# Attention and two MoE layers in one kernel: the second MoE with four pairs of chunks by seven products, groups of 4, 4 and 8, integer turns for the cosine, and half the second sums added by DMA

## The chip, the core and the metric

The kernel is written in Bass and Tile for Trainium2 and runs on one core. A core has TensorE (PE, matmuls; PEld is its weight load), VectorE (DVE), ScalarE (ACT), GpSimd (POOL) and SyncE (SP, which here only starts transfers). The metric is the time of one execution on the device, in microseconds; lower is better.

## What is computed

Causal attention with a decay bias over 4 batches, 8 heads and 576 positions gives 2304 tokens of 512 numbers. They go through two layers with a hidden width of 2048. Only the second is changed:

```python
def _moe_ref(x, w_in, w_out):
    h = np.maximum(x @ w_in, 0.0)
    return (h * h @ w_out).astype(np.float32)

def _moe2_ref(x, w_in, w_out):
    h = x @ w_in
    g = h * np.cos(h)
    return (g @ w_out).astype(np.float32)
```

with w_in 512 x 2048 and w_out 2048 x 512.

## The kernel before

The order of all instructions is written out by hand (`manual_schedule`): each engine runs its instructions in the order in which the program emits them.

**The second MoE.** The 2304 tokens are cut into blocks 0 to 4 (`blocks`: four of 512 tokens, the last of 256), the hidden width into 16 chunks f of 128. A value is kept as a high and a low half of 16 bits, so a product of two values is three matmuls (`PASSES`). `m2_g1(j, f)` multiplies block j by the columns of chunk f: 12 matmuls of 512 columns (256 for block 4) into the PSUM tile hp. `m2_cos` and `m2_sin` make cos(h) from it as a sine of whole turns removed, `m2_mul` multiplies by h, `m2_high` and `m2_rest` split the result g into gh and gl. `m2_g2` multiplies g by chunk f of w_out: for each 128 tokens a of the block 3 matmuls of 512 columns into PSUM tile o0 to o3.

**Groups.** Chunks are worked off in three groups (`GROUPS`, here numbered 1 to 3; in the code p = 0, 1, 2). Within a group all blocks are done one after the other. After the last chunk of a group for a block, the four o tiles are evicted, scaled by `osc`: group 1 writes them to the tiles `part` in SBUF, group 2 adds to these (four times on DVE, line 1678), group 3 adds the rest (o0 and o2 on DVE; o1 and o3 by ACT into `os` and POOL's addition, line 1684) and stores the rows. `part[c]` and `half[c]` are the two halves of the tile that holds weight entry c.

**Pairs.** From chunk `PAIR0` on, blocks 0 to 3 take two chunks at once, in `unit`: a scheme of seven products of half-sized blocks instead of eight (`PROD`), each 6 matmuls of 256 columns into a PSUM bank. `snap` copies a bank to SBUF on ACT, `join` adds a bank to it on DVE. Product 6 adds to the bank that was snapped after product 1, product 5 to that, product 3 to that; so each waits for the snap before. Block 4 takes all its chunks singly. The combined columns of the weights are made by `pair_high` (additions on DVE into the tile `sums`, conversions on ACT) and `w_lo`; the combined rows of the tokens by `t_make`, a few instructions at each `t_tick`.

**The loop** goes over `items`, one chunk (or pair) of one block each. An item emits `m2_g1` of its chunk, the cosine, the high half of the item before, weight conversion, the sine, the low half (gl) of the item before, then `m2_g2` of the chunk two items back (`fifo`, `G2LAG`), then more weight conversion and the multiplication. A unit has two places for output products: `first` and `second` are the oldest chunks in the fifo, each cut into `out_part(x, 0)` (its first half of the o tiles) and `out_part(x, 1)`.

**Weights.** The queue `wq` lists 64 entries, 32 of them of the second MoE: (1, f, a), a = 0 for w_in, 1 for w_out. An entry is loaded, clipped on ACT (line 975), shifted and combined on DVE (lines 981 and 985), squared on ACT for its scale, and then converted to a high half on ACT (1008, 1034) and a low half on DVE (1051, 1042). `goal` says how many entries shall have passed line 985 by item i; eight are done when the second MoE begins, and the rate is `P_BITS`, later `LATE_BITS`, per item. In the first MoE's last block the raw entries are loaded as that layer's weights come free, at each of its output chunks f except even ones from `PAIR0` on.

Of the kernel before, what the change touches and what calls it, by code (L numbers as in the profile page):

```python
# [30 lines left out]
GROUPS = ((0, 4), (4, 9), (9, 16))  # L31
PAIR0 = 10
T_FROM = 20
LATE_BITS = 0.62
RAWS = 6
NB2 = 5
LAG = (3, 5)
# [78 lines left out]
P_BITS = 0.75  # L116
QUIET = 3
PAUSE = 14
# [14 lines left out]
def attention_moe_moe_kernel(  # L133
# [64 lines left out]
    wq += [(1, f + m, a) for f in range(PAIR0, NF, 2) for a in range(2) for m in range(2)]  # L198
# [811 lines left out]
    def pair_high(j, m):  # L1010
# [5 lines left out]
        if m == 0:  # L1016
            q = p2q[0].tile([128, KD, BT], F32, tag="yr", bufs=2, name="sums")
# [493 lines left out]
    for k in range(NB1):  # L1511
# [41 lines left out]
        if k == NB1 - 2:  # L1553
# [6 lines left out]
            for name, shape, t in (  # L1560
                ("onesb", [128, 128], BF16),
                ("wss", [128, 2 * NF], F32),
# [17 lines left out]
            nc.vector.memset(sm["onesb"], 1.0)  # L1580
            nc.vector.memset(sm["ysm"], 0.0)
# [34 lines left out]
    def m2_cos(j, f, p=2):  # L1616
        n = blocks[j][1]
        hp = hd2[j, f]
        a = p2.tile([128, n], F32, tag="a", bufs=2, name="a")
        kf = p2.tile([128, n], F32, tag="kf", bufs=2, name="kf")  # L1620
        nc.scalar.activation(out=a, in_=hp, func=ACTF.Copy, scale=sm["hsc"][:, j, f:f + 1], bias=0.25)
        if p == 1:
            nc.scalar.activation(out=kf, in_=a, func=ACTF.Copy, bias=MAGIC)
            nc.vector.scalar_tensor_tensor(
                out=kf, in0=kf, scalar=MAGIC, in1=a, op0=ALU.subtract, op1=ALU.subtract
            )
            hd2[j, f] = (hp, a, kf)
            return
        nc.vector.tensor_scalar(out=kf, in0=a, scalar1=MAGIC, scalar2=MAGIC, op0=ALU.add, op1=ALU.subtract)
        nc.vector.tensor_tensor(out=kf, in0=kf, in1=a, op=ALU.subtract)  # L1630
        hd2[j, f] = (hp, a, kf)

    def m2_sin(j, f):
        hp, a, kf = hd2[j, f]
        nc.scalar.activation(out=a, in_=kf, func=ACTF.Sin, scale=-6.2831850)  # L1635
        hd2[j, f] = (hp, a)
# [22 lines left out]
    def m2_g2(p, j, f, pick=None):  # L1659
# [4 lines left out]
        sc = sm["osc"][:, p, j:j + 1]  # L1664
        if first:
            ops.setdefault(j, {})
        for a in range(n // 128) if pick is None else pick:
# [7 lines left out]
            if last:  # L1675
                st = part[4 * j + a]
                if p == 1 or p and (a % 2 == 0 or j == NB2 - 1):
# [3 lines left out]
                elif p:  # L1681
                    os = p2.tile([128, DM], F32, tag="os", bufs=2, name="os")
# [102 lines left out]
    def unit(j, f, prev):  # L1785
# [23 lines left out]
        if old:  # L1809
            m2_high(*old[0])  # L1810
            m2_mul(*old[1])
# [39 lines left out]
    for i, (kind, p, j, f) in enumerate(items):  # L1851
# [33 lines left out]
        if i > G2LAG and prev[0] == "f":  # L1885
            m2_rest(*prev[1:])
# [76 lines left out]
```

## Time and profile before

| | |
|---|---|
| median of 3 runs | 972.91 us (971.38 to 973.18) |
| the profiled execution | 972.91 us, span of its instructions 970.8 us |
| PE busy | 937.3 us, 97% |
| DVE busy | 769.7 us, 79% |
| ACT busy | 709.7 us, 73% |
| POOL busy | 159.9 us, 16% |
| second MoE | first hp matmul at 595.2 us, last o matmul at 965.4 us |

The span runs from the first instruction to the last; the execution takes some 2 us more. Matmuls are pipelined: a matmul's own duration overlaps that of the next, so what the PE needs for one is read from the distance between starts, or from a piece of the chain that counts several.

### The profile page before, as it was taken

To read this page: it belongs to the slowest core of one execution; us is meant where nothing else is said; L and a number is where in the kernel's file an instruction comes from. 1 tells how busy PE (TensorE), PEld (TensorE's weight loads), DVE (VectorE), ACT (ScalarE), POOL (GpSimd) and SP (SyncE) were. 2 spreads that over 40 slices of the span, in tenths; PEclk is the share of its full clock that TensorE was granted. 3 is DMA by queue.
4 is the path that set the end of the run, shared out by engine and by line. 5 is a ranking of instruction groups with operands and counts; after the bars stand their busy time and mean duration, and the time that the engine had idled before them with its cause. 6 is when DMAs were issued, how large, how long until landed. Compare 5 with 4: busy or idle time off the path is not lost.

```text
span 970.8 us, 21039 instructions
## 1 busy us (share of the span) xinstructions
PE 937.3 (97%) x7474; PEld 726.9 (75%) x7474; DVE 769.7 (79%) x1944; ACT 709.7 (73%) x1625; POOL 159.9 (16%) x298
## 2 busy tenths in 40 slices
PE   6999999989999999999999999999999999999997
PEld 5899998988989988999989986445544456666664
DVE  6899986789798866787997375888788788798774
ACT  6799887878898767676776686677777666565553
POOL 2001123222211222222330022430000000001101
PEclk9999999999999999999999999999999999999999
DMA  8984799657998987589999679210000000112001
GB/s 246 312 271 149 168 213 227 168 145 151 200 183 191 204 195 170 134 177 174 211 215 158 217 267 362 66 44 23 1 1 1 22 1 22 49 60 67 23 22 66
DMA packets 158074, 135.38 MB, mean 139 GB/s; under 512 B 109272, under 2 KB 132128, under 8 KB 157968
## 3 DMA queue, kind: packets, MB, share of 16 engines
q1 hardware_dynamic: 147664, 123.78, 50.8%
q0 software_dynamic: 10304, 10.24, 5.2%
q8 instruction: 59, 0.97, 0.4%
q14 instruction: 47, 0.39, 0.1%
HBM read 93.91 MB, written 15.83 MB: 113 GB/s over the span
## 4 chain that ended last, share of the span: by engine, by line
PE 59%; DVE 6%; ACT 3%; issue 2%; DMA 2%; SPq 0%; DVEq 0%; ACTq 0%
PE o L1671 18%; PE hp L1610 12%; PE y L1197 11%; PE hps L1165 9%; PE bank L1762 5%; PE qkp L567 2%; PE pvs L697 2%; DVE k L415 1%; DVE sb L585 1%; DMA raw<-in_qk_dram 1%; DMA rw<-in_w_dram 1%; DMA vb<-v_d 1%; DVE wt L1678 1%; PE xps L752 0%; ACT sb L608 0%
## 5 line engine op out<-in xcount | busy, mean ns | idle before, releaser
L1197 PE MATMUL y<-gh,wt 128*128 128x256 f32 x1152 | 237.7, 289 | 0.0
L1197 PEld LDWEIGHTS y<-gh,wt 128*128 128x128 f32 x1152 | 188.6, 190 | 1.2
L1671 PE MATMUL o<-wt,gh 128*128 128x512 f16 x576 | 171.3, 379 | 1.5 <-ACT gh L1649 1.3
L1197 PE MATMUL y<-gl,wt 128*128 128x256 f32 x576 | 162.9, 283 | 0.5 <-DVE gl L1187 0.5
L1165 PE MATMUL hps<-xh,w 128*128 128x256 f16 x1152 | 142.0, 273 | 2.6 <-ACT g L1177 2.4
L1610 PE MATMUL hp<-yh,wt 128*128 128x512 f16 (+1 forms) x448 | 124.9, 348 | 0.0
L1165 PEld LDWEIGHTS <-w 128*128 128x128 f16 x1152 | 106.1, 98 | 17.8 <-issue 4.2
L1197 PEld LDWEIGHTS y<-gl,wt 128*128 128x128 f32 x576 | 109.9, 191 | 1.4 <-DVE gl L1187 0.9
L1671 PE MATMUL o<-wt,gl 128*128 128x512 f16 x288 | 109.2, 379 | 0.0
L1610 PEld LDWEIGHTS <-wt 128*128 128x128 f16 x672 | 63.9, 98 | 59.1
L1671 PEld LDWEIGHTS <-gh 128*128 128x128 f16 x576 | 56.3, 98 | 56.3 <-ACT gh L1649 1.6
L608 ACT ACTIVATE sb<-sb 128x128 f32<-128x128 f32 (+7 forms) x152 | 87.4, 575 | 4.9 <-DVE sb L585 4.3
L1177 ACT ACTIVATE g<-hps,sc 128x256 f32<-128x256 f32 x96 | 45.1, 470 | 61.3 <-PE hps L1165 59.8
L397 POOL DMA_DIRECT2D k<-ext_d x80 | 41.1, 514 | 260.2 <-PE qkp L567 159.3
L1165 PE MATMUL hps<-xh,wt 128*128 128x256 f32 x384 | 81.4, 294 | 0.3 <-ACT g L1179 0.2
L1187 DVE TENSOR_TENSOR gl<-g,gh 128x256 fp32r<-128x256 f32 x144 | 61.3, 426 | 22.8 <-ACT gh L1181 14.7
L1610 PE MATMUL hp<-yl,wt 128*128 128x512 f16 (+1 forms) x224 | 78.0, 348 | 0.0
L585 DVE CUSTOM_DVE_ANT_0 sb<-qkp,mask 128x128 f32<-128x128 f32 (+7 forms) x152 | 69.3, 456 | 5.3 <-PE qkp L552 4.3
L656 DVE SCALAR_TENSOR_TENSOR p<-sb,p 128x384 f16<-128x384 f32 (+3 forms) x120 | 66.3, 553 | 8.8 <-ACT p L650 5.6
L1635 ACT ACTIVATE a<-kf 128x512 f32<-128x512 f32 (+1 forms) x80 | 46.5, 583 | 31.4 <-DVE kf L1630 30.4
L405 ACT CAST hi<-raw 128x704 fp32r<-128x704 f32 (+2 forms) x80 | 58.8, 735 | 13.6 <-DMA raw<-in_qk_dram 7.2
L1165 PEld LDWEIGHTS hps<-xh,wt 128*128 128x128 f32 x384 | 64.5, 195 | 2.8 <-issue 1.2
(172 smaller groups left out, 2006.8 us busy)
## 6 DMA issues: line engine op xcount, KB each, us to landing
rw<-in_w_dram SPq DMA_DIRECT2D x64, 512.0 KB
raw<-in_qk_dram SPq DMA_DIRECT2D x48, 352.0 KB
yr<-y_d SPq DMA_DIRECT2D x17, 512.0 KB
raw<-in_qk_dram SPq DMA_DIRECT2D x16, 384.0 KB
v_d<-vt SPq DMA_DIRECT2D x16, 320.0 KB
vb<-v_d SPq DMA_DIRECT2D x32, 160.0 KB
vr<-in_v_dram POOLq DMA_DIRECT2D x15, 320.0 KB, 5.4
y_d<-yst SPq DMA_DIRECT2D x18, 256.0 KB
```

What stands on the lines that cost most here:

```text
L405: nc.scalar.copy(hi[:, BT - nq:BT + nk], raw[:, BT - nq:BT + nk])
L585: nc.vector.tensor_tensor_reduce(out=sb[0:r, c0:c0 + cn], in0=p[0:r, 0:cn], in1=mask[0:r, mo:mo + cn], scale=-0.125, scalar=(3.0e38 if k = ...
L608: nc.scalar.activation(out=sb[0:r, 0:w], in_=sb[0:r, 0:w], func=ACTF.Exp, scale=-1.0, bias=j["nb"], accum_out=z[0:r, ti, x:x + 1],)
L656: nc.vector.scalar_tensor_tensor(out=p[0:r, cw:cw + w], in0=sb[0:r, 0:w], scalar=PSC, in1=p[0:r, 0:w], op0=ALU.mult, op1=ALU.subtract,)
L1165: nc.tensor.matmul(hp, w[:, a, c * 128:(c + 1) * 128], (xh, xl)[e][:, c, :], start=(n == 0), stop=(n == 3 * KD - 1),)
L1177: nc.scalar.activation(out=g, in_=hp, func=ACTF.Relu, scale=hs1[:, f // 2:f // 2 + 1])
L1187: nc.vector.tensor_tensor(out=gl, in0=g, in1=gh, op=ALU.subtract)
L1197: nc.tensor.matmul(yps[k][d // 2][:, d % 2, :], w[:, a, d * 128:(d + 1) * 128], (gh, gl)[e], start=(f == 0 and n == 0 and d % 2 == 0), sto ...
L1610: nc.tensor.matmul(hp, chunk_of(w, a, c), (yh, yl)[e][:, c, :], start=(m == 0), stop=(m == 3 * KD - 1),)
L1635: nc.scalar.activation(out=a, in_=kf, func=ACTF.Sin, scale=-6.2831850)
L1671: nc.tensor.matmul(ops[j][a], (gh, gl)[e][:, a * 128:(a + 1) * 128], w[:, x, :], start=(first and m == 0), stop=(last and m == 2),)
L1762: nc.tensor.matmul(bank[b][:, 0:HB], w[:, a, wx, c * 128:(c + 1) * 128], y_side(j, yx, e, c), start=(start and n == 0), stop=(n == 5), ski ...
```

## The change

- `GROUPS` goes from 4, 5, 7 chunks to 4, 4, 8, and `PAIR0` from 10 to 8. So group 3 of blocks 0 to 3 is four pairs, with no single chunk before them.
- The queue of weights takes w_out before w_in for the first pair; `PARTS` names the 18 tiles that hold the partial sums, since chunks 8 and 9 now have such a tile only beside their w_out.
- Weight entries are converted at 1.05 an item in group 1 and 0.68 in group 2, only in blocks 0 to 3, and not in group 3.
- `m2_cos`: ACT writes the number of turns as an integer, one step on DVE subtracts it from the scaled h (two before; in group 2 two ACT steps and one DVE step). The sine takes the quarter turn as a bias tile.
- Evictions are no longer emitted within `m2_g2` but collected in `evq2` and emitted by `m2_evict`, after other work in a unit. In group 2, o1 and o3 of blocks 0 to 3 go by ACT into tile `os` and are added to `part` by an accumulating DMA from POOL's queue; o0 and o2, and block 4, stay on DVE.
- `os` has one buffer in group 3, shared with `sums`; in group 2 it takes the buffers of `yr`.
- In a unit the snap after product 6 comes before the high half of the old chunk, and both ticks of `t_make` after the join of product 5.

```diff
-GROUPS = ((0, 4), (4, 9), (9, 16))
-PAIR0 = 10
+GROUPS = ((0, 4), (4, 8), (8, 16))
+PAIR0 = 8
-LATE_BITS = 0.62
+BITS2 = (1.05, 0.68, 0)
+PARTS = (*range(2 * PAIR0), 2 * PAIR0 + 1, 2 * PAIR0 + 3)
...
-    wq += [(1, f + m, a) for f in range(PAIR0, NF, 2) for a in range(2) for m in range(2)]
+    wq += [(1, f + m, a) for f in range(PAIR0, NF, 2) for a in ((1, 0) if f == PAIR0 else (0, 1)) for m in range(2)]
...
-            q = p2q[0].tile([128, KD, BT], F32, tag="yr", bufs=2, name="sums")
+            q = p2q[1].tile([128, KD, BT], F32, tag="os", bufs=1, name="sums")
...
-    def m2_cos(j, f, p=2):
+    def m2_cos(j, f):
...
+        sc = sm["hsc"][:, j, f:f + 1]
...
-        nc.vector.tensor_scalar(out=kf, in0=a, scalar1=MAGIC, scalar2=MAGIC, op0=ALU.add, op1=ALU.subtract)
-        nc.vector.tensor_tensor(out=kf, in0=kf, in1=a, op=ALU.subtract)
+        kf = p2.tile([128, n], I32, tag="kf", bufs=2, name="kf")
+        nc.scalar.activation(out=kf, in_=hp, func=ACTF.Copy, scale=sc, bias=0.25)
+        nc.vector.scalar_tensor_tensor(out=a, in0=hp, scalar=sc, in1=kf, op0=ALU.mult, op1=ALU.subtract)
...
-        nc.scalar.activation(out=a, in_=kf, func=ACTF.Sin, scale=-6.2831850)
+        nc.scalar.activation(out=a, in_=a, func=ACTF.Sin, scale=6.2831850, bias=sm["hpi"])
...
             if last:
-                st = part[4 * j + a]
-                if p == 1 or p and (a % 2 == 0 or j == NB2 - 1):
+                evq2.append((p, j, f, a))
+    def m2_evict():
+        while evq2:
+            p, j, f, a = evq2.pop(0)
...
+                st = part[PARTS[4 * j + a]]
+                if p and (a % 2 == 0 or j == NB2 - 1):
                     nc.vector.scalar_tensor_tensor(
                         out=st, in0=ops[j][a], scalar=sc, in1=st, op0=ALU.mult, op1=ALU.add
                     )
                 elif p:
...
                     nc.scalar.activation(out=os, in_=ops[j][a], func=ACTF.Copy, scale=sc)
-                    nc.gpsimd.tensor_tensor(out=st, in0=os, in1=st, op=ALU.add)
+                    if p == 1:
+                        nc.gpsimd.dma_start(out=st, in_=os, accum_op=ALU.add)
+                    else:
+                        nc.gpsimd.tensor_tensor(out=st, in0=os, in1=st, op=ALU.add)
...
         join(j, f, 1, 0, 0)
+        m2_evict()
         out_part(first, 0)
...
         prod(j, f, 6, 0, False)
+        snap(j, f, 0, 1, 0)
+        m2_evict()
         if old:
             m2_high(*old[0])
             m2_mul(*old[1])
-        snap(j, f, 0, 1, 0)
         prod(j, f, 7, 2, True)
         out_part(first, 1)
         if old:
             m2_high(*old[1])
             m2_rest(*old[0])
             m2_rest(*old[1])
-            t_tick(j + 1)
         prod(j, f, 5, 0, False)
         snap(j, f, 0, 1, 1)
         join(j, f, 2, 1, 1)
+        m2_evict()
+        if old:
+            t_tick(j + 1)
         out_part(second, 0)
...
-        k = i + 1 - QUIET
-        goal = min(4 * NF, bits0 + int(max(0, min(k, PAUSE)) * P_BITS) + int(max(0, k - PAUSE - 1) * LATE_BITS))
+        if i >= QUIET and j < NB2 - 1:
+            pace[0] += BITS2[p]
+        goal = min(4 * NF, bits0 + int(pace[0]))
```

## Rows read from the trace of the kernel before

**Rows 1.** Busy time by stretch: PE, PEld, DVE, ACT, POOL, clock, DMA share, GB/s

```profile
595.20:683.80 88.60, 88.60 (x442) 42.10 (x441) 72.26 (x129) 61.08 (x118) 21.54 (x17) 1.00 0.24 84
788.00:826.00 38.00, 36.03 (x242) 22.77 (x239) 32.55 (x77) 24.27 (x52) 0.00 (x0) 1.00 0.05 15
826.00:965.80 139.80, 139.57 (x894) 87.16 (x891) 104.88 (x186) 79.79 (x152) 10.11 (x8) 1.00 0.14 46
```

**Rows 2.** Chain of waits: start us, us, what; 512 columns, then 256

```profile
605.75 2.59 PE hp L1610 x12
...
857.99 1.31 PE bank L1762 x12
```

**Rows 3.** Timeline of PE: start us, us, what, idle before

```profile
797.39 0.59 PE L1671 MATMUL o<-wt,gh 128*128 128x512 f16 x2 [0.18 <-DVE wt L1678]
...
799.92 0.27 PE L1610 MATMUL hp<-yh,wt 128*128 128x256 f16 x1
801.52 0.60 PE L1671 MATMUL o<-wt,gh 128*128 128x512 f16 x2 [1.33 <-ACT gh L1649]
...
813.41 0.82 PE L1762 MATMUL bank<-wt,wt 128*128 128x256 f16 x6
814.69 0.27 PE L1762 MATMUL bank<-yh,wt 128*128 128x256 f16 x1 [0.46 <-ACT hs L1772]
...
855.47 0.38 PE L1671 MATMUL o<-wt,gl 128*128 128x512 f16 x1
855.88 0.82 PE L1762 MATMUL bank<-wt,wt 128*128 128x256 f16 x6
```

**Rows 4.** Groups by line and shape in the second MoE: count, busy us, mean ns

```profile
L1656 DVE TENSOR_TENSOR gl<-a,gh 128x512 f16<-128x512 f32 x64 | 44.0, 687 | 3.9 <-ACT gh L1649 2.7
L1630 DVE TENSOR_TENSOR kf<-kf,a 128x512 f32<-128x512 f32 x44 | 36.9, 839 | 1.5
L1641 DVE SCALAR_TENSOR_TENSOR a<-hp,gsc,a 128x512 f32<-128x512 f32 x40 | 29.9, 747 | 8.9 <-ACT a L1635 8.8
L1629 DVE TENSOR_SCALAR kf<-a 128x512 f32<-128x512 f32 x44 | 21.4, 485 | 9.4 <-ACT a L1621 8.3
L1772 ACT COPY hs<-bank 128x256 f32<-128x256 f32 x48 | 17.7, 369 | 27.6 <-PE bank L1762 26.9
L1621 ACT ACTIVATE a<-hs,hsc 128x512 f32<-128x512 f32 x24 | 17.2, 722 | 0.4
L1776 DVE TENSOR_TENSOR hs<-bank,hs 128x256 f32<-128x256 f32 x36 | 15.2, 422 | 20.8 <-ACT hs L1772 10.2 <-PE bank L1762 10.0
L1624 DVE SCALAR_TENSOR_TENSOR kf<-kf,a 128x512 f32<-128x512 f32 x20 | 13.8, 690 | 16.1 <-ACT kf L1623 15.9
L1051 DVE SCALAR_TENSOR_TENSOR wt<-st,wsc,wt 128x512 f16<-128x512 f32 x18 | 12.7, 747 | 0.3 <-ACT wt L1008 0.3
L1623 ACT ACTIVATE kf<-a 128x512 f32<-128x512 f32 x20 | 12.6, 630 | 0.6
L1684 POOL TENSOR_TENSOR wt<-os,wt 128x512 f32<-128x512 f32 x8 | 10.1, 1269 | 287.5 <-ACT os L1683 256.6 <-DVE wt L1708 30.9
```

**Rows 5.** Timeline of DVE: start us, us, the four evictions of block 3, group 2

```profile
796.59 2.72 DVE L1678 SCALAR_TENSOR_TENSOR wt<-o,osc,wt 128x512 f32<-128x512 f32 x4
```

**Rows 6.** Timeline of POOL and of DVE in block 2 of group 1

```profile
643.92 2.65 POOL L1253 TENSOR_TENSOR yl<-yr,yh 128x512 f16<-128x512 f32 x2 [8.29 <-ACT yh L1252]
...
645.49 1.37 DVE L1629 TENSOR_SCALAR kf<-a 128x512 f32<-128x512 f32 x1 [0.38 <-ACT a L1621]
646.89 1.49 DVE L1630 TENSOR_TENSOR kf<-kf,a 128x512 f32<-128x512 f32 x1
```

**Rows 7.** Timeline of ACT and of DVE in group 2: hp taken up, gl made

```profile
722.85 0.69 ACT L1621 ACTIVATE a<-hp,hsc 128x512 f32<-128x512 f32 x1 [2.54 <-PE hp L1610]
...
727.71 0.69 DVE L1656 TENSOR_TENSOR gl<-a,gh 128x512 f16<-128x512 f32 x1
```

**Rows 8.** DMA issues: line, count, KB each, median us to landing

```profile
vr<-in_v_dram POOLq DMA_DIRECT2D x15, 320.0 KB, 5.4
```

More of the change, by code (lines that the diff above doesn't have):

```diff
@@ L1614, in m2_g1 @@
         hd2[j, f] = hp
-    def m2_cos(j, f, p=2):
+    def m2_cos(j, f):
         n = blocks[j][1]
         hp = hd2[j, f]
+        sc = sm["hsc"][:, j, f:f + 1]
         a = p2.tile([128, n], F32, tag="a", bufs=2, name="a")
[L1620 to L1628, printed above, removed]
-        nc.vector.tensor_scalar(out=kf, in0=a, scalar1=MAGIC, scalar2=MAGIC, op0=ALU.add, op1=ALU.subtract)
-        nc.vector.tensor_tensor(out=kf, in0=kf, in1=a, op=ALU.subtract)
-        hd2[j, f] = (hp, a, kf)
+        kf = p2.tile([128, n], I32, tag="kf", bufs=2, name="kf")
+        nc.scalar.activation(out=kf, in_=hp, func=ACTF.Copy, scale=sc, bias=0.25)
+        nc.vector.scalar_tensor_tensor(out=a, in0=hp, scalar=sc, in1=kf, op0=ALU.mult, op1=ALU.subtract)
+        hd2[j, f] = (hp, a)
     def m2_sin(j, f):
-        hp, a, kf = hd2[j, f]
-        nc.scalar.activation(out=a, in_=kf, func=ACTF.Sin, scale=-6.2831850)
-        hd2[j, f] = (hp, a)
+        hp, a = hd2[j, f]
+        nc.scalar.activation(out=a, in_=a, func=ACTF.Sin, scale=6.2831850, bias=sm["hpi"])
     def m2_mul(p, j, f):
@@ L1675, in m2_g2 @@
             if last:
-                st = part[4 * j + a]
-                if p == 1 or p and (a % 2 == 0 or j == NB2 - 1):
+                evq2.append((p, j, f, a))
+    evq2 = []
+    def m2_evict():
+        while evq2:
+            p, j, f, a = evq2.pop(0)
+            t0, n = blocks[j]
+            sc = sm["osc"][:, p, j:j + 1]
+            if True:
+                st = part[PARTS[4 * j + a]]
+                if p and (a % 2 == 0 or j == NB2 - 1):
                     nc.vector.scalar_tensor_tensor(
@@ L1681, in m2_g2 @@
                 elif p:
-                    os = p2.tile([128, DM], F32, tag="os", bufs=2, name="os")
+                    if p == 1:
+                        os = p2q[0].tile([128, KD, BT], F32, tag="yr", bufs=2, name="os")
+                    else:
+                        os = p2.tile([128, KD, BT], F32, tag="os", bufs=1, name="os")
+                    os = os[:, 0:2].rearrange("p a c -> p (a c)")
                     nc.scalar.activation(out=os, in_=ops[j][a], func=ACTF.Copy, scale=sc)
-                    nc.gpsimd.tensor_tensor(out=st, in0=os, in1=st, op=ALU.add)
+                    if p == 1:
+                        nc.gpsimd.dma_start(out=st, in_=os, accum_op=ALU.add)
+                    else:
+                        nc.gpsimd.tensor_tensor(out=st, in0=os, in1=st, op=ALU.add)
                 elif a % 2 == 0:
@@ L1690, in m2_g2 @@
                 for row, x, m in _pieces(t0 + a * 128, 128):
-                    nc.sync.dma_start(out=out[row:row + m, :], in_=part[4 * j + a][x:x + m])
+                    nc.sync.dma_start(out=out[row:row + m, :], in_=part[PARTS[4 * j + a]][x:x + m])
     HB = BT
@@ L1828, in unit @@
         join(j, f, 2, 1, 0)
+        m2_evict()
         for m in range(2):
@@ L1886, in attention_moe_moe_kernel @@
             m2_rest(*prev[1:])
+        m2_evict()
         if len(fifo) >= G2LAG:
             m2_g2(*fifo.pop(0))
+            m2_evict()
         if p == 0 and j + 1 < NB2 and f == 1:
@@ L1913, in attention_moe_moe_kernel @@
         m2_g2(*fifo.pop(0))
+        m2_evict()
 def _lay_out(inputs):
```

9 lines of the change are left out of this document (4 added, 5 removed).

## The prediction

> **What bounds the kernel now.** I read the stretches of the second MoE first, because the change touches nothing else but an order of weight loads. In the first group of chunks the PE is busy in all 88.60 us, from 826 to 965.8 us in 139.57 of 139.80; only between 788 and 826 us does it miss about 2 us (36.03 of 38.00) [rows 1]. The granted clock is 1.00 throughout, the 2.4 GHz level [rows 1], so no time is to be had from the clock. The chain of waits agrees: one piece of PE work follows the other, 2.59 us for twelve matmuls over 512 columns, 1.31 us for twelve over 256 columns [rows 2]. So this stage is worth what its matmuls are worth, plus the places where the PE stands still. DVE (72.26) and ACT (61.08 us of 88.60) matter only where their lateness reaches the PE [rows 1].
>
> I then looked for those places by the spacing of the matmuls' starts. There are three kinds. Around the change from the second to the third group: a 256-column matmul starts at 799.92 and the next only at 801.52, where 0.11 was due, so 1.5 us are lost, and 0.18 before 797.39 [rows 3]; with two slivers beside them some 2.0 us. In the first unit of seven products: at 813.41 six matmuls start (0.66 us of work) and the next starts at 814.69: 0.6 us lost, waiting for ACT's snap [rows 3]. And in one unit of each of three blocks a bank matmul that was due 0.22 after 855.47 starts 0.41 after it: 0.2 us, three times, some 0.6 [rows 3]. Together about 3.2 us, of which the first 2.0 is a jam of DVE: four evictions stand in one row, 2.72 us from 796.59, in items that are only half as long as the others because block 4 has 256 tokens [rows 5].
>
> **The change, part by part.**
>
> *A fourth pair.* For each of blocks 0 to 3, chunks 8 and 9 go from 24 matmuls of 512 columns to 7 x 6 = 42 of 256. At 2.59 and 1.31 per twelve [rows 2] that is 5.18 against 4.585 us: 0.6 us a block, 2.4 us in all, and it lies wholly on the path, since the PE is the path. The output products stay as many. The three pairs of before already run at this spacing, so it is no guess. Each pair adds four snaps (0.369) on ACT and three joins (0.422) on DVE [rows 4], 2.7 us per block, beside 9.8 us of PE in a unit.
>
> *Cosine by integer turns.* In groups 1 and 3 DVE drops a tensor_scalar (0.485) and a tensor_tensor (0.839) for one scalar_tensor_tensor. The trace has none with an int32 operand and a scalar; nearest is the multiplication by the same accumulator, 0.747 [rows 4]; below it the bound is 0.690 (the fused step of group 2), above it 0.839 [rows 4]. I take 0.747: DVE saves 0.58 per chunk of 512. In group 2 ACT drops one pass of 0.630 [rows 4], DVE pays 0.06 more. The sine gets a bias by pointer; the row of a cosine step with a pointer, 0.722 [rows 4], bounds it at 0.1 more than now. None of this is on the path by itself: it shortens the chain from hp to the output product by some 0.5 us a chunk, and the chain has slack already.
>
> The two dropped steps took 1.37 and 1.49 us while POOL worked from 643.92 to 646.57, 0.9 and 0.7 more than their usual time [rows 4, 6]. The Trainium skill's SBUF — State Buffer (Who interferes with whom) says why: a DVE instruction with two SBUF inputs, or in a two-port mode, is shut out for as long as a GpSimd instruction that reads SBUF runs. The trace agrees so far. By that page the new step is free of it in single chunks (hp lies in PSUM) and not in pairs; the sum is the same by either, and what it would do in pairs is rival 2.
>
> *Faster weights.* By item 15 thirteen entries are converted, not nine, and none in group 3. An entry costs DVE three passes, each at most 0.747 (the step of line 1051 [rows 4]), so at most 2.2, and ACT three passes of about 0.72, 2.2 as well. Four more entries are 9 us on each. DVE gets 13 x 0.58 = 7.5 back; ACT gets nothing, and with 61.08 of 88.60 busy it goes to some 80% in blocks 0 to 3. Is that late enough to reach the PE? The item at 722.85 of before measures the slack: its hp was ready then, gl of the chunk before it was made from 727.71 on, and the PE was to use it after two more pieces of 2.59, at about 728.0 [rows 2, 7]. DVE was some 2.2 us behind there, four additions for a pair stood before gl, and no wait of the PE is listed. So an item can bear DVE 3 to 3.6 us behind. The heavy items of group 1 have cosine, multiplication and gl (2.2), two evictions (half of 2.72 [rows 5]), two low halves and two passes for an entry (0.75 each): 6.6 us on DVE against 5.2 of PE; the light ones between them, without evictions and low halves, 3.7. So DVE gets 1.4 behind and takes it back. Tightest are items 17 and 18, half-sized with the first pair's conversion in them: 17 has 1.4 for its own steps, 1.4 of evictions, four additions (0.42) and 1024 columns of low halves (1.5), 6.0 us against 3.9 of PE; 18 has 2.9 against 2.6. That is 2.4 behind, where a half-sized item bears about 2.6. I enter 0.2 us for that place.
>
> *The change from group 2 to group 3.* Entries end before block 4 of group 2, the last pair's conversion lies in items 35 and 36, and of four evictions two go to ACT and a DMA. So the 2.0 us jam goes. Late next is the first unit: it has only one chunk in the fifo to spare, so product 5 is followed at once by product 3, and the same snap as at 814.69 keeps its 0.6 us. And then there is a new wait in the second unit. There "first" is the last chunk of block 4 (group 2) and "second" the first chunk of block 0 (group 3), which needs the same o banks. m2_evict puts the eviction of o1 behind both gl and join(2, 1, 1). By the durations of rows 4 and 5, counted from the unit's start: two cosine steps to 2.0, join 2.35, multiplication 3.0, eviction of o0 3.7, multiplication 4.3, two gl 5.6, join 6.0, eviction of o1 6.7 us. The PE, whose two output parts are half as long with block 4, wants o1 at 5.2. So it waits 1.5 us (bounds: 0.5 if DVE gets ahead by one pass of 0.75 and a bit more, 2.5 if a pass slips the other way). Queued behind that wait on the PE: the rest of that unit, nothing else.
>
> *Snap first, evictions later.* ACT's snap now stands before the high halves, which were what it waited behind at 855.47. That takes the three 0.2 us away. In the second units of blocks 1 to 3 the last chunk of the old and the first of the new block also meet. The same count gives the PE's wants at 5.9, 6.5, 8.5 and 9.2 us, and the evictions' ends at 3.8, 4.4, 7.6 and 7.0. Close, not late; I enter 0.1 each, 0.3. The ticks for the next block move behind the eviction; their loads start when the last low half is done, some 8 us before their first use.
>
> *Half the second sums by DMA.* Eight transfers of 256 KB, issued by POOL. The trace has no accumulating DMA; nearest is a load of 320 KB by the same queue, 5.4 us [rows 8]. Their sums are next read in group 3, some 100 us later, so ten times that would be hidden; POOL has nothing else in group 2. Their source tiles come back after four items, 20 us. What can hurt is ACT, which in block 0 must wait for the y parts that t_make still uses: that is item 25, and I enter 0.2.
>
> **Sum.** The profiled execution took 972.91 us, which is also the median (971.38 to 973.18); its span is 970.8. 972.9 - 2.4 (matmuls) - 2.0 (jam) - 0.6 (three snaps) + 1.5 (o1) + 0.2 + 0.3 + 0.2 = 970.1. The 0.6 of the first unit, the start and the 5 us after the last matmul stay.
>
> **Rivals.**
> 1. *No new wait.* If DVE is ahead in the second unit and the four small entries are nought, all but the 0.6 goes: 972.9 - 2.4 - 2.6 = 967.9. For it: each DVE pass gained counts; against it: the order in the queue is fixed and the count is 1.5 us over. 13%.
> 2. *The gain is eaten at the block changes.* In the second unit of each block the eviction of o2 ends 0.9 us before it is wanted, by my count. The new cosine step of a pair reads hs and kf, both in SBUF, as gl does, and POOL adds two halves of 1.3 us there. If each addition delays DVE by 0.8 [rows 4, 6], the three units lose 0.7 each instead of 0.1, and if items 17 and 18 lose as little as that too: 970.1 + 1.8 = 971.9, no change. The Trainium skill's page named above speaks for this one: by it, POOL shuts out the new step in these units just as it did the removed one. 22%.
> 3. *Slower: DVE falls behind under the faster weights.* Place: blocks 1 and 2 of group 1, where POOL works 2.65 us at a stretch [rows 6]. Price: four more entries, 9 us, and the steps with two SBUF inputs held up through 0.6 of POOL's 21.54 us [rows 1], 13 us; less 7.5 saved: 14.5. DVE has 16.3 us idle in the group [rows 1], about half of it in block 0, where conversion only begins. So it would be 14.5 - 8 = 6.5 us short in the rest, of which some 1 is made up in the half-sized items. It decides from the point at which DVE is 3.6 us behind. 972.9 - 2.4 - 2.6 + 2.2 + 5.4 = 975.5. Against it: gl (0.687 mean of 64 [rows 4]) and the weights' steps show no such delay in the means now; only the two removed steps do. 10%.
>
> That the seven products save nothing I leave out; the three pairs show their price.
>
> **How the numbers follow.** Forecast 970.1, chance 55%, own range 969.0 to 971.4. About 0.2%, 1.95 us, is what a measurement of this kernel can tell from no change: faster means below 970.96. Seven eighths of the forecast's case lie there, 48%, and all of rival 1, 13%: 61% faster. Same: the rest of the forecast, 7%, and rival 2, 22%: 29%. Slower 10%. The range takes in rivals 1 and 2 with the runs' own spread: 967.8 to 973.2.
>
> **What would show it.** Right: 576 hp matmuls where there were 672 and 672 bank matmuls where there were 504; no loss in the half-sized items of group 2; one wait of the PE for an eviction of DVE of 1 to 2 us in the second unit; the 0.6 of the first unit still there; DVE's busy time down by some 20 us. Wrong: losses inside group 1 or in items 17 to 25 (rival 3), a wait of the PE for evictions in three more units (rival 2), or none in the second unit (rival 1).

## The result and the profile after

The changed kernel takes 976.31 us (median of 6 runs, 976.04 to 977.79), the kernel before 971.29 us beside it (6 runs, 969.45 to 973.18): a ratio of 1.0052, with an interval of 1.0039 to 1.0065. It is slower by about 5 us, where 2.8 less than the profiled run of before had been forecast.

The stretch that the change touches is told apart from the rest by the trace: "stage" below is the time from the start of the first hp matmul to the start of the last o matmul. In before it is 370.23 us (595.22 to 965.45), in after 377.52 us (592.74 to 970.26), 7.3 us more. Outside it, the profiled run of before took longer than all the others: 972.91 - 370.23 = 602.7, where the eleven kernels below have 596.4 to 601.3 and after 598.7. Its stage began later (the first hp matmul at 595.22, in after at 592.74), and 5.4 us passed from its last o matmul's start to the end of the span, 4.2 in after. So the forecast stood on a base that was 1.3 to 2.1 us high (972.9, against medians of 970.8 to 971.6 in later runs), and the stage is what is to be compared. There is one profile of each kernel; why the medians differ by 5.0 us where the stages differ by 7.3 is not shown by the runs.

Busy time of after by stretch, with the columns of [rows 1]; the first three answer to its three rows, the last two lie where after stands still longest:

```profile
592.70:681.30 88.60, 87.99 (x438) 41.15 (x437) 70.87 (x134) 65.91 (x128) 21.27 (x17) 1.00 0.26 94
785.00:823.00 38.00, 35.85 (x252) 24.35 (x251) 28.32 (x59) 22.95 (x46) 0.59 (x1) 1.00 0.17 43
823.00:968.00 145.00, 145.00 (x970) 94.48 (x968) 96.28 (x162) 85.72 (x167) 10.16 (x8) 1.00 0.13 44
...
718.00:721.50 3.50, 1.53 (x7) 0.61 (x6) 1.88 (x6) 0.69 (x1) 0.91 (x1) 0.94 0.00 0
721.50:727.50 6.00, 3.60 (x9) 1.14 (x8) 1.59 (x3) 3.50 (x6) 0.86 (x1) 0.50 0.46 79
```

From 823 us on, the PE never stands still; the losses lie ahead of that. The last row is new: in these 6 us the granted clock is 0.50, the 1.2 GHz level, where before had 1.00 in all its stretches [rows 1]. PE's timeline of after at the four places (start us, us, what, idle before and its releaser):

```profile
684.07 0.27 PE L1611 MATMUL hp<-yh,wt 128*128 128x256 f16 x1
684.85 0.60 PE L1663 MATMUL o<-wt,gh 128*128 128x512 f16 x2 [0.50 <-ACT gh L1642]
...
717.98 0.38 PE L1663 MATMUL o<-wt,gl 128*128 128x512 f16 x1
720.32 0.59 PE L1663 MATMUL o<-wt,gh 128*128 128x512 f16 x2 [1.97 <-ACT os L1689]
...
721.71 0.63 PE L1663 MATMUL o<-wt,gl 128*128 128x512 f16 x1
724.74 1.01 PE L1663 MATMUL o<-wt,gh 128*128 128x512 f16 x2 [2.40 <-ACT os L1689]
...
725.97 0.63 PE L1611 MATMUL hp<-yh,wt 128*128 128x512 f16 x1
726.40 0.63 PE L1611 MATMUL hp<-yl,wt 128*128 128x512 f16 x1
...
783.68 0.59 PE L1663 MATMUL o<-wt,gh 128*128 128x512 f16 x2 [0.46 <-DVE wt L1680]
...
787.17 0.39 PE L1663 MATMUL o<-wt,gl 128*128 128x512 f16 x1 [0.29 <-DVE gl L1649]
...
793.42 0.27 PE L1771 MATMUL bank<-yh,wt 128*128 128x256 f16 x1 [0.46 <-ACT hs L1781]
...
799.87 0.39 PE L1663 MATMUL o<-wt,gl 128*128 128x512 f16 x1
801.63 0.59 PE L1663 MATMUL o<-wt,gh 128*128 128x512 f16 x2 [1.37 <-DVE wt L1680]
```

Read as in [rows 3], by the distance between starts less what is due (0.216 for 512 columns, 0.109 for 256), the losses are:

- group 1, six places between 647 and 685 us, 2.3 us together; the row at 684.85 is the largest (0.67);
- item 25, the first block of group 2: 2.12 and 2.81 us, both behind os, and 0.31 between them, where the matmuls are already slow;
- behind it, until 728 us, 1.5 us: matmuls of 512 columns start 0.43 apart (725.97 to 726.40) instead of 0.216;
- the change from group 2 to group 3: 0.61, 0.45 and a 0.19 at 788.6, 1.25 us in all;
- the first unit 0.62, the second unit 0.14 and 1.54.

That is some 12.7 us, against 3.5 in before.

What holds the PE at 720 and at 724 stands in the timelines of ACT, POOL and DVE:

```profile
719.59 0.69 ACT L1689 ACTIVATE os<-o,osc 128x512 f32<-128x512 f32 x1 [2.60 <-DVE wsm L1075]
724.00 0.69 ACT L1689 ACTIVATE os<-o,osc 128x512 f32<-128x512 f32 x1 [3.73 <-DMA wt<-os]
...
720.58 0.91 POOL L1691 DMA_DIRECT2D wt<-os  x1 [65.17 <-ACT os L1689]
...
718.73 0.74 DVE L1723 SCALAR_TENSOR_TENSOR wt<-yr,ysc,wt 128x512 f16<-128x512 f32 x1
...
725.91 0.75 DVE L1624 SCALAR_TENSOR_TENSOR a<-hp,hsc,kf 128x512 f32<-128x512 f32 x1 [5.97 <-ACT kf L1623]
```

By the kernel's code the two os tiles take the two buffers of yr. One of them is still held by t_make, so both go through the other. The first os waits until t_make's low half (718.73, done at 719.47) has read that buffer; DVE comes to it only behind the evictions and a multiplication. The second os waits until the accumulating DMA has taken the first one out: ACT stands for 3.73 us, and the eviction of o3 with it. The profile names L1075, a small scale step right behind it, as the first releaser; the buffer's own reader is the L1723 row. All that is queued behind os on ACT, the next cosine's first step (725.20) among it, comes late, so DVE idles 5.97 us.

### The profile page after: what moved, and what is told of

It is laid out like the page before. It is cut to its first block, busy times and chain, and to the rows that moved or that the text cites. A ratio compares the mean times of both kernels' runs of the same rounds, so it can differ in the third digit from the quotient of the medians.

```text
span 974.5 us, 21104 instructions
## 1 busy us (share of the span) xinstructions
PE 937.3 (96%) x7548; PEld 732.8 (75%) x7548; DVE 753.9 (77%) x1901; ACT 710.7 (73%) x1627; POOL 166.7 (17%) x306
## 4 chain that ended last, share of the span: by engine, by line
PE 53%; issue 9%; DVE 8%; ACT 4%; DMA 2%; POOL 0%; DVEq 0%; SPq 0%; ACTq 0%; POOLq 0%
PE o L1663 13%; PE y L1196 11%; PE hps L1164 10%; PE bank L1771 7%; PE hp L1611 6%; PE qkp L566 2%; PE pvs L696 2%; DVE k L414 1%; DVE sb L584 1%; DVE st L984 1%; DMA raw<-in_qk_dram 1%; DVE a L1634 1%; DMA pt<-p 1%; DMA rw<-in_w_dram 1%; ACT wt L1007 1%
## 5 line engine op out<-in xcount | busy, mean ns | idle before, releaser
L1611 PE MATMUL hp<-yh,wt 128*128 128x512 f16 (+1 forms) x384 | 105.2, 345 | 0.0
L1611 PEld LDWEIGHTS <-wt 128*128 128x128 f16 x576 | 55.0, 98 | 48.7 <-issue 1.9
L1771 PEld LDWEIGHTS <-wt 128*128 128x128 f16 x672 | 65.7, 98 | 21.6 <-issue 0.8
L1611 PE MATMUL hp<-yl,wt 128*128 128x512 f16 (+1 forms) x192 | 66.3, 345 | 0.0
```

What stands on the lines that cost most here:

```text
L1611: nc.tensor.matmul(hp, chunk_of(w, a, c), (yh, yl)[e][:, c, :], start=(m == 0), stop=(m == 3 * KD - 1),)
L1771: nc.tensor.matmul(bank[b][:, 0:HB], w[:, a, wx, c * 128:(c + 1) * 128], y_side(j, yx, e, c), start=(start and n == 0), stop=(n == 5), ski ...
```

## The experiments

All kernels stood beside runs of before. "Stage" is the stretch defined above, from one profile each.

| kernel | median us | ratio to before (interval) | stage us |
|---|---|---|---|
| before | 970.8 to 971.6 | 1 | 370.23 |
| after | 976.31 | 1.0052 (1.0039 to 1.0065) | 377.52 |
| e1, t_make two items earlier | 970.10 | 0.9996 (0.9980 to 1.0012) | 370.61 |
| e2, group 2 evicted by DVE alone | 972.29 | 1.0014 (1.0000 to 1.0027) | 372.32 |
| e3, slower weights in group 1 | 976.22 | 1.0061 (1.0046 to 1.0076) | 376.49 |
| e5, o1 evicted earlier | 976.93 | 1.0081 (1.0052 to 1.0110) | 376.53 |
| e6, e1 + slower in group 1, faster in 2 | 971.52 | 1.0010 (0.9994 to 1.0026) | 371.96 |
| e7, before + integer cosine | 969.28 | 0.9985 (0.9974 to 0.9996) | 369.14 |
| e8, e1 + order of the second unit | 969.64 | 0.9982 (0.9971 to 0.9994) | 370.03 |
| e9, e1 + old cosine | 976.05 | 1.0061 (1.0047 to 1.0074) | 376.36 |
| e11, three mends, rates 0.85 and 0.81 | 966.35 | 0.9947 (0.9932 to 0.9962) | 367.27 |
| e12, three mends, rates 0.90 and 0.78 | 965.92 | 0.9944 (0.9928 to 0.9959) | 367.33 |
| e13, e12 + join ahead of gl | 966.06 | 0.9943 (0.9923 to 0.9962) | 366.26 |

**e1: t_make two items earlier.**

```diff
-T_FROM = 20
+T_FROM = 18
```

> The changed kernel with one number undone the other way: the making of the combined token columns for block 0 starts at item 18 instead of 20, so that it has let go of both yr buffers before the first evictions of group 2 ask for them (item 25). Nothing is left out. Theory A (the os tiles of block 0 wait for t_make and then for each other's DMA, because both go through one free buffer; and the low granted clock that follows is a consequence of the two stops): the PE's two losses of 2.1 and 2.8 us between 718 and 725 us go, the granted clock stays at 1.00 through 721 to 728 us, which gives back another 1.8 us; some 6.5 to 7 us less than the changed kernel's 976.3, about 969.5. Theory B (the accumulating DMA itself, or the weight work in these items, stops the PE): the stop stays where it is, 976 us. Theory C (the clock falls for a reason of its own): the two stops go, the clock still falls, about 971.4. The steps of t_make now lie in the half-sized items 18 and 19; a loss there of up to 1 us would show.

Theory A, nearly to the number: 970.10 us, 6.2 less than after where it had 6.5 to 7; the stage is 6.9 shorter. Busy time in the same two stretches:

```profile
718.00:721.50 3.50, 3.50 (x18) 1.55 (x16) 3.46 (x7) 3.50 (x7) 0.58 (x1) 1.00 0.90 155
721.50:727.50 6.00, 6.00 (x29) 2.73 (x28) 4.07 (x7) 2.53 (x6) 0.00 (x0) 1.00 0.01 1
```

and the last output products and the evictions of block 0 in the timelines of PE and ACT:

```profile
717.64 0.38 PE L1663 MATMUL o<-wt,gl 128*128 128x512 f16 x1
717.85 0.59 PE L1663 MATMUL o<-wt,gh 128*128 128x512 f16 x2
...
715.79 1.25 ACT L1689 ACTIVATE os<-o,osc 128x512 f32<-128x512 f32 x2
```

Now both os run one behind the other at 715.79, each into its own buffer. The two DMAs are still there, with the DMA share at 0.90 from 718 to 721.5, and no matmul waits. So the transfer itself costs the PE nothing; the buffer did. And with no stops the clock stays at 1.00, so the 1.8 us lost at 0.50 (1.5 and the 0.31) were a consequence of them, not a cause of its own. The half-sized items 18 and 19 lose nothing by t_make's steps: the losses in group 1 stay at 2.3.

**e2: group 2 evicted by DVE alone.**

```diff
-                if p and (a % 2 == 0 or j == NB2 - 1):
+                if p == 1 or p and (a % 2 == 0 or j == NB2 - 1):
```

> The changed kernel with all four evictions of group 2 on DVE as before the change, no os tile and no DMA in that group. Nothing is left out. Theory A (the two stops in item 25 are the wait for the yr buffers): both stops and the low clock go, since nothing asks for a yr buffer; DVE has 8 more passes of 0.68 us in blocks 0 to 3 of group 2, which lies beside other work, so 969.5 to 971. Theory B (DVE is short in group 2 after the faster weights, and the DMAs were needed): new losses at the block changes of group 2, 0.5 to 1 us each, 972 to 974. Theory C (the stop is the weight conversion's): unchanged, 976.

Stops and low clock go here too (1.00 in both stretches), which agrees with the buffer as the cause. But the time is 972.29, 2.2 above e1, in theory B's range, though not where B put it: two block changes lose 0.13 and 0.17, and most comes at the change to group 3. There the third chunk's gl is 1.55 us late, where e1 loses 0.46:

```profile
782.18 0.39 PE L1663 MATMUL o<-wt,gl 128*128 128x512 f16 x1 [1.38 <-DVE gl L1649]
```

So the sums by DMA are worth about 2 us (2.2 in the medians, 1.7 in the stage), as long as their source tiles have buffers.

**e3: slower weights in group 1.**

```diff
-BITS2 = (1.05, 0.68, 0)
+BITS2 = (0.80, 0.90, 0)
```

> The changed kernel with the weight entries at 0.80 an item in group 1 and 0.90 in group 2, instead of 1.05 and 0.68; the last entry is done in the same item. Nothing is left out. Theory A (the five small losses in group 1, 2.3 us together, come from the three more entries there): they fall to below 0.7 us, the two stops of item 25 stay, some 1.5 us less than the changed kernel: 974.5 to 975; if the entries that move into group 2 cost there what they cost in group 1, 975 to 976.3. Theory B (the losses in group 1 come from the new cosine step or the order of the evictions): they stay at 2.3 us, 976.3. Theory C (the weights cause the stop of item 25): it changes its length by more than 1 us.

Each theory has a part. Group 1 loses nothing any more (the first row: PE busy 88.60 of 88.60), as A said. But the time does not move, and the stage is only 1.0 shorter: item 25 now loses 3.14 and 2.12, with 1.0 of slow matmuls between them; a gl behind it loses 0.93, and one os in a later block 0.65. The PE reaches item 25's first stop 2.5 us earlier in the stage than in after, but t_make's low half, which frees the buffer, comes only 1.5 earlier: at the new rates a weight entry's steps stand ahead of it on DVE (714.62 to 717.01). So 1.0 of what group 1 gave was waited away at the next stop, whose length hangs on DVE's weight work too, a part of theory C. From the first os to the second it is 4.4 us, as in after. Busy time of group 1, and PE's timeline of item 25:

```profile
593.10:681.70 88.60, 88.60 (x442) 42.08 (x442) 65.69 (x123) 62.71 (x119) 21.03 (x17) 1.00 0.26 93
```

```profile
715.90 0.38 PE L1663 MATMUL o<-wt,gl 128*128 128x512 f16 x1
719.26 1.01 PE L1663 MATMUL o<-wt,gh 128*128 128x512 f16 x2 [2.99 <-ACT os L1689]
...
723.69 0.59 PE L1663 MATMUL o<-wt,gh 128*128 128x512 f16 x2 [1.71 <-ACT os L1689]
```

**e5: o1 evicted earlier in the second unit.**

```diff
         out_part(first, 1)
+        if first and first[0] == 1:
+            m2_evict()
         if old:
```

> The changed kernel with one call added: in the second unit of block 0 the eviction of o1 stands right behind the output products that finish it, ahead of the two gl and of the join of product 5, as the kernel before had it. Nothing is left out. Theory A (the 1.5 us that the PE loses at 800 us are the place of that eviction in DVE's order): the loss falls below 0.5 us, the time by 1.1 to 1.5 us to about 975; the gl that now stand behind it are wanted later and cost at most 0.3. Theory B (DVE is late as a whole there, and whatever stands last is late): the loss turns up at the next wait, for gl or the join, and the time stays at 976.3.

The loss falls from 1.54 to 0.80, and the wait that is left is for gl, as theory B said. By the timeline DVE runs from 796.47 to 801.57 without a gap, until the second gl is done, so moving one step only names another. The 0.7 us do not show in the times: the median is 976.93, after's 976.31.

**e7: the integer cosine alone, on the kernel before.** Its edit is the part of the diff that concerns `m2_cos`, `m2_sin` and `hpi`.

> The kernel before with the integer cosine alone (the new cosine and sine steps in all three groups); groups, pairs, weights, evictions as before. Nothing is left out. Theory A, that of the prediction (the cosine is on the path by itself only where DVE is late): the three losses of 0.2 stay, the jam of 2.0 us at the change to group 3 shrinks by a few passes of 0.5, the rest is unchanged: 0.2 to 1.0 us less than before, 970.0 to 970.8 where before has 971.0. Theory B (the new step is slow or collides with POOL): 971.5 or more, new losses in group 1. As a second look at the kernel up to the second MoE, which is the same as before: its first hp matmul should be at 592.5 to 594 us if the 595.2 of the profiled run of before was only a late run.

It gains 1.5 us (0.4 to 2.5 by the interval), somewhat more than theory A said, and in other places: the three losses of 0.2 that A left standing are gone, while the jam keeps 1.82 of its 2.0 us. Its first hp matmul is at 592.83, so before's 595.22 was a late start, as e6's 594.97 and e12's 595.15 were. The new step takes 750 ns from PSUM and 757 from SBUF, beside 747 for the multiplication [rows 4], which was the row it had been costed by:

```profile
L1625 DVE SCALAR_TENSOR_TENSOR a<-hp,hsc,kf 128x512 f32<-128x512 f32 x40 | 30.0, 750 | 31.0 <-ACT kf L1624 30.7
...
L1625 DVE SCALAR_TENSOR_TENSOR a<-hs,hsc,kf 128x512 f32<-128x512 f32 x24 | 17.6, 757 | 1.0
```

**e9: the old cosine on e1.** The float turns of before, in all three groups; in before itself, group 2 has two ACT steps and one DVE step in their place.

> The changed kernel with t_make for block 0 from item 18 on, but with the old cosine (float turns, two DVE steps, in all three groups). Nothing is left out. To be compared with 970.1 us. Theory A (group 1 is bound by the weight pace, and the integer step pays for a part of it): DVE has 0.58 us more a chunk, about 11.6 us in group 1 beside three more entries: the losses of group 1 grow from 2.3 to 5 us or more, and those at the change to group 3 by 0.5 to 1: 973 to 976. Theory B (group 1's losses are ACT's, which has as many cosine passes as before): the losses grow by less than 1 us, 970 to 971.

Theory A, at the upper end of its range: 976.05, 6 us above e1. Group 1 loses 5.8 us instead of 2.3, the change to group 3 2.2 instead of 1.25, the second unit 2.4 instead of 1.7, and one os of block 0 in group 2 loses 0.6. So the integer cosine is worth 1.5 us on the kernel before and 6 in the changed one. The two edits are not the same in group 2; 3.5 of the 6 lie in group 1, where they are.

**e6: e1 with 0.80 in group 1 and 1.0 in group 2.**

```diff
-BITS2 = (1.05, 0.68, 0)
+BITS2 = (0.80, 1.0, 0)
```

> The changed kernel with t_make for block 0 from item 18 on, and the weight entries at 0.80 an item in group 1 and 1.0 in group 2, so that the last entry is done two items earlier than in the changed kernel. Nothing is left out. With t_make early alone 970.1 us were measured; the slower pace took away the 2.3 us of group 1 but the stop of item 25 swallowed them. Theory A (the three causes are separate: os buffers, weight pace in group 1, DVE at the change from group 2 to 3): now both gains stand, the 2.3 us of group 1 go, and of the 1.25 at the change to group 3 some 0.6 to 1.0 goes, since the last conversions lie earlier: 966.9 to 967.8. Theory B (the entries cost the same wherever they are put): what group 1 gives back is lost again in blocks 1 to 3 of group 2, at the block changes; 969.5 to 970.5.

Theory B, and beyond it (971.5 where it had 969.5 to 970.5; one of the twelve runs took 2362.84 us, for a reason that is not known, and without it the median is 971.10): group 1 loses nothing, and group 2 now loses 4.4 us before its block 4, at these places in PE's timeline:

```profile
721.05 0.16 PE L1068 MATMUL stat<-wss,onesb 128*128 128x1 bf16 x1 [1.03 <-DVE wsm L1075]
...
735.24 0.39 PE L1663 MATMUL o<-wt,gl 128*128 128x512 f16 x1 [0.47 <-DVE gl L1649]
...
741.07 0.59 PE L1663 MATMUL o<-wt,gh 128*128 128x512 f16 x2 [0.81 <-DVE wt L1680]
...
757.71 0.39 PE L1663 MATMUL o<-wt,gl 128*128 128x512 f16 x1 [0.45 <-DVE gl L1649]
...
763.54 0.59 PE L1663 MATMUL o<-wt,gh 128*128 128x512 f16 x2 [0.82 <-DVE wt L1680]
```

At one entry an item, the entry's steps also fall on the items that have the evictions, and two of the waits are for an eviction (741.07, 763.54). At the change to group 3 it is as theory A said: 0.52 is lost there, where e1 loses 1.36.

**e8: the order of the second unit, on e1.**

```diff
         m2_evict()
+        swap = first and first[0] == 1
         if old:
             m2_high(*old[0])
-            m2_mul(*old[1])
+            (m2_rest(*old[0]) if swap else m2_mul(*old[1]))
...
         out_part(first, 1)
-        if old:
+        if old and swap:
+            m2_evict()
+            m2_mul(*old[1])
+        if old:
             m2_high(*old[1])
-            m2_rest(*old[0])
+            if not swap:
+                m2_rest(*old[0])
             m2_rest(*old[1])
```

> The changed kernel with t_make for block 0 from item 18 on, and in the second unit of block 0 another order on DVE: the gl of the chunk that comes next stands right behind the eviction of o0, then the eviction of o1, and the multiplication and gl of the other chunk after them. Nothing is left out. To be compared with 970.1 us (t_make early alone). Moving o1's eviction alone took the wait from 1.54 to 0.80 us and handed the rest to gl. Theory A (only what stands ahead of the two steps that the PE waits for matters): DVE has 2.0 for two cosine steps, join, multiplication, eviction, gl, eviction to do, 5.1 us after the unit's start, where the PE wants them at 5.2: the wait falls below 0.4 us, 968.7 to 969.2. Theory B (DVE comes late into this unit from the one before, whatever the order): 0.8 us stay, 969.4 or more.

Both waits, for o1 and for gl, are gone, and a new one of 0.93 stands behind them: the snap after product 5 now comes behind a high half on ACT, which waits for the multiplication that was put off. So neither theory holds as written. DVE had enough time for what the PE wants; the delayed step dragged ACT's queue with it. 969.64 is 0.5 below e1, which the times alone don't separate.

**e11 and e12: three mends together.** e1's line, an even rate of the weights, and e8's order with that high half and gl moved behind the snap:

```diff
-T_FROM = 20
-BITS2 = (1.05, 0.68, 0)
+T_FROM = 18
+BITS2 = (0.85, 0.81, 0)
...
         out_part(first, 1)
-        if old:
+        if old and swap:
+            m2_evict()
+            m2_mul(*old[1])
+        elif old:
             m2_high(*old[1])
             m2_rest(*old[0])
             m2_rest(*old[1])
         prod(j, f, 5, 0, False)
         snap(j, f, 0, 1, 1)
+        if old and swap:
+            m2_high(*old[1])
+            m2_rest(*old[1])
         join(j, f, 2, 1, 1)
```

> The changed kernel with three mends: t_make for block 0 from item 18 on; the weight entries at an even rate, 0.85 an item in group 1 and 0.81 in group 2; in the second unit of block 0 gl of the next chunk and the eviction of o1 ahead of the other chunk's multiplication, and that chunk's high half behind the snap after product 5. Nothing is left out. Theory A (both groups have room for some entries, and only the excess stops the PE: no loss in group 2 at 0.68, none in group 1 at 0.80): group 1 falls from 2.3 to below 0.7 us, group 2 loses below 0.5, the second unit below 0.3 instead of 1.54; 966.5 to 967.5. Theory B (what is taken out of one group comes back in the other, us for us): 969 to 970.

> As the kernel with the three mends, but with the entries at 0.90 in group 1 and 0.78 in group 2, nearer to the changed kernel's 1.05 and 0.68. Nothing is left out. Theory A (only the excess over some rate costs): within 0.7 us of the kernel with 0.85 and 0.81, the losses in group 1 between 0.3 and 1.2 us, those in group 2 below 0.3. Theory B (us for us): the same sum of losses in other places, 969 to 970.

Theory A: 966.35 and 965.92, both faster than before by 0.5 to 0.6%; e11 is 0.15 below the range that it had. Group 1 loses nothing in either (e12 had been given 0.3 to 1.2 there), group 2 nothing in e11 and 0.19 in e12. The large miss is in the second unit, 1.07 us for the join that now stands behind gl.

**e13: the join ahead of gl.**

```diff
         if old and swap:
             m2_high(*old[1])
-            m2_rest(*old[1])
         join(j, f, 2, 1, 1)
+        if old and swap:
+            m2_rest(*old[1])
```

> The kernel with the three mends and the rates 0.90 and 0.78 (965.9 us), with one step moved: in the second unit of block 0 the join of product 5 stands ahead of the second chunk's gl, not behind it. Nothing is left out. There the PE loses 1.07 us before product 4, whose bank is the one that this join must empty. Theory A (the wait is the place of the join in DVE's order): the loss goes below 0.2, gl ends 0.3 later and is wanted only in the next unit; about 965.0. Theory B (DVE is late as a whole, and the next step takes the wait over): a loss of 0.5 us or more turns up behind it in the same or the next unit; 965.5 to 966.

In the trace theory A: no wait of the PE is left in the second unit, none follows it, and the stage is 366.26, 1.1 less than e12's. The medians, 966.06 against 965.92, don't show it, and by themselves are nearer to theory B's 965.5 to 966. Busy time by stretch of this kernel, four stretches of the stage:

```profile
592.60:681.20 88.60, 88.60 (x442) 42.06 (x441) 68.93 (x126) 64.19 (x123) 20.69 (x17) 1.00 0.26 94
690.00:770.00 80.00, 79.96 (x402) 37.59 (x401) 72.43 (x140) 61.02 (x116) 5.25 (x6) 1.00 0.12 20
770.00:802.00 32.00, 31.06 (x218) 20.95 (x216) 25.89 (x59) 20.73 (x42) 1.72 (x2) 1.00 0.20 50
802.00:959.00 157.00, 157.00 (x1046) 101.79 (x1044) 104.48 (x177) 92.10 (x179) 10.16 (x8) 1.00 0.12 41
```

## Why the prediction was wrong, point by point

| term of the sum | predicted | in after's trace |
|---|---|---|
| matmuls of the fourth pair | -2.4 | -2.0 |
| jam at the change to group 3 | -2.0 | -0.7 |
| three snaps of 0.2 | -0.6 | -0.7 |
| o1 in the second unit | +1.5 | +1.5 |
| items 17 and 18; all of group 1 | +0.2 | +2.3 |
| three block changes in units | +0.3 | 0 |
| item 25, with the slow matmuls behind it | +0.2 | +6.8 |

**The step that failed is item 25.** The text named the place, that ACT must wait there for the y parts that t_make still uses, and entered 0.2. Measured were 2.12 for that wait, 2.81 for a second one that the sum had at nothing, behind the transfer, and 1.8 at the low clock. The text failed in two of its sentences. "Their source tiles come back after four items" is true of all blocks but the first, where one of the two buffers is not there at all, so two evictions in a row share the other. And "ten times that would be hidden" looked at who reads the sums, not at who waits for the buffer that the transfer empties. The nearest row was in hand: 5.4 us for 320 KB [rows 8]. With one buffer such a transfer stands between two evictions: 4.41 us from the first os to the second (719.59 to 724.00). Measured, in the list of DMA issues of after (KB each, median us from issue to landing):

```profile
wt<-os POOLq DMA_DIRECT2D x8, 256.0 KB, 3.4
```

The Trainium skill's DMA: Bandwidth & Descriptors (Anatomy of one DMA — SWDGE (gpsimd) path) gives 2.0 us plus bytes at 436 GB/s for a transfer by GpSimd's queue, 2.6 us here as an estimate; these accumulating ones took 3.4, and the measurement decides.

**The clock had no place in the sum.** The text took from [rows 1] that it is 1.00 throughout and that no time is to be had. It could be lost. The price was 1.8 of the 6.8 us, and e1 shows that it goes with the stops. Before's own trace has a stretch at 0.50, 3.4 us from 160.6 on (0.66 over 160 to 165), ahead of the stage and so outside the rows that were read.

**Group 1 is rival 3's mechanism at a part of its price.** The text set it aside because gl and the weights' steps showed no delay in their means. In before the removed cosine steps stood there instead [rows 6]. Its other ground, that an item can bear DVE 3 to 3.6 us behind, rests on a misread item: the text found no wait of the PE near 728.0, but the gl matmul there starts 0.20 late (PE's timeline of before; it was due 0.43 after the two gh), just behind gl, done at 728.40. So DVE was at the limit there:

```profile
727.83 0.59 PE L1671 MATMUL o<-wt,gh 128*128 128x512 f16 x2
728.46 0.39 PE L1671 MATMUL o<-wt,gl 128*128 128x512 f16 x1
```

Groups of DVE by line in group 1 of before, then of after, where L1656, L985 and L981 are L1649, L984 and L980 (count, busy us, mean ns, idle before):

```profile
L1656 DVE TENSOR_TENSOR gl<-a,gh 128x512 f16<-128x512 f32 x16 | 11.0, 685 | 1.4 <-ACT gh L1649 1.4
...
L985 DVE SCALAR_TENSOR_TENSOR st<-rw,st 128x512 int32<-128x512 int32 x10 | 6.9, 692 | 0.3
...
L981 DVE TENSOR_SCALAR st<-st 128x512 int32<-128x512 int32 x10 | 4.2, 420 | 0.0
```

```profile
L1649 DVE TENSOR_TENSOR gl<-a,gh 128x512 f16<-128x512 f32 x16 | 12.2, 763 | 1.8 <-ACT gh L1642 1.7
L1624 DVE SCALAR_TENSOR_TENSOR a<-hp,hsc,kf 128x512 f32<-128x512 f32 x16 | 11.9, 746 | 6.3 <-ACT kf L1623 6.3
L1634 DVE SCALAR_TENSOR_TENSOR a<-hp,gsc,a 128x512 f32<-128x512 f32 x16 | 11.9, 745 | 2.4 <-ACT a L1629 2.4
L984 DVE SCALAR_TENSOR_TENSOR st<-rw,st 128x512 int32<-128x512 int32 x13 | 11.5, 882 | 0.4
L980 DVE TENSOR_SCALAR st<-st 128x512 int32<-128x512 int32 x13 | 7.5, 577 | 4.8 <-ACT st L974 4.7
```

In after 13 x 0.190 + 13 x 0.157 + 16 x 0.078 = 5.8 us are time by which these steps are longer than in before, in the blocks in which POOL works. The steps that read hp from PSUM stay at 746 and 745. The split is the one that the Trainium skill's SBUF — State Buffer (Who interferes with whom) states for DVE steps with two SBUF inputs or in a two-port mode; the trace agrees. The forecast had applied that page to the steps that go and to the new one in pairs, not to those that then stand beside POOL. The runs show both sources: the cosine alone, at the old rate (e7), takes the two weight steps to 764 and 504 ns with no loss of the PE, the fast weights with the old cosine (e9) to 882 and 683. At 11 entries (e12) they are at 781 and 497, and the PE loses nothing. So it decides between 11 and 13 entries, and costs 2.3 us, not rival 3's 5.4. In the rows above DVE also waits 4.7 us for ACT's clips, and ACT's evictions and gh are what the PE's rows name; which of the two engines is late first is not settled by these runs, though with more work for DVE alone (e9) the loss grows from 2.3 to 5.8.

**The jam.** Entries do end before block 4, and two of four evictions do leave DVE, worth about 2 us (e2). What was not counted is what the last entries leave behind: the last pair's low halves come just ahead of the evictions, and the scale steps of group 3 right behind them, in the half-sized items of block 4. DVE's timeline of after:

```profile
780.26 1.02 DVE L1041 SCALAR_TENSOR_TENSOR wt<-sums,wsc,wt 128x768 f16<-128x768 f32 x1 [0.76 <-ACT wt L1033]
...
782.89 1.40 DVE L1680 SCALAR_TENSOR_TENSOR wt<-o,osc,wt 128x512 f32<-128x512 f32 x2
...
784.60 0.15 DVE L1075 TENSOR_SCALAR wsm<-stat 128x2 f32<-128x2 f32 x1
...
786.19 0.21 DVE L1126 TENSOR_SCALAR osc<-yin,wil 128x1 f32<-128x1 f32 x1
```

Thirteen small steps, 784.60 to 786.40, are 1.8 us in a place where an item of the PE has 2.6. That these steps are the cause is read from the order of the timeline; the run that bears on it is e6, where the last entry is done two items earlier and 0.52 is left of the loss.

**What was right.** The forecast wait in the second unit: 1.54 for 1.5, for the eviction that was named, by a count of DVE's queue from row durations; e5 and e8 show that the queue's order was indeed the cause. As forecast, the stage has 576 hp matmuls and 672 bank matmuls, where there were 672 and 504. DVE's busy time fell by 15.8 us (769.7 to 753.9), not by some 20. The first unit's 0.62 stays. The 0.2 us of the three snaps go, though e7 shows that the cosine alone takes them away too. The matmuls save 2.0 of 2.4, by the stage less its losses: 366.7 in before and e7, 364.6 to 364.8 in after, e1, e12 and e13. The spacing of the matmuls is the forecast's (0.216 and 0.109 us, which gives 2.4); the rest is in gaps too small to be listed, most of them between output products. Rival 2, collisions at the block changes, happens and costs nothing: POOL's additions stretch one gl to 1.35 us at each of three block changes, not the new cosine step (0.754 at most), and no wait of the PE follows (DVE's timeline of after at the first of them):

```profile
839.14 1.35 DVE L1649 TENSOR_TENSOR gl<-a,gh 128x512 f16<-128x512 f32 x1 [0.98 <-ACT gh L1642]
```

The cosine's duration stood on the right row.

**Luck.** That e1, with item 25 mended, comes out at the forecast's 970.1 is chance: group 1 and the jam still cost 3.4 us more than the sum had, and the base was 1.9 lower than the 972.9 that it started from.

## What to carry to other kernels

A transfer that nobody waits for can still be waited for by its source: count the buffers in the item where the loan begins, not in the steady state, and price each further use of one buffer at issue plus landing. A step that is taken out from beside a conflicting engine hands its place to the next step; cost that one at the collided duration. When a change moves work off its slack in several places, mend one place alone and the gain may be lost again at the next, in part to waiting and in part to the work that was moved there (e3): here the same change went from 0.5% slower to 0.6% faster by three changes of its order and rates.

## What had not been expected of the hardware

The granted clock fell to 0.50, the 1.2 GHz level, near 721.1, after one stop of the PE of 2.1 us and 0.7 us of work (it is 0.94 over 718.00 to 721.50, and the matmul at 721.71, ahead of the second stop, already takes 0.63 instead of 0.38). It stayed there through the stop of 2.8 us until 727.9 (0.80 over 727.50 to 728.50), 6.8 us in all. In e3, after one stop of 3.1 us, the matmuls at 719.26 to 721.35 were slow, and at 723.69, after a further stop, they were at full speed again. Stops of 1.5 us, alone (801.63), cost no clock. What decides between them was not tried. And a DVE step with an int32 operand, a pointer scale and an f32 result takes the time of a float one: 746 against 745 ns in group 1 of after.
